# Second product of the first MLP as seven block products in eight steps

## The chip, the cores and the metric

The kernel runs on one core of one Trainium2 chip. The metric is device time in microseconds of one execution; the time before is the median of three runs. A profile is one further execution, recorded by the hardware profiler. Engines are named as the profile names them: PE (TensorE), DVE (VectorE), ACT (ScalarE), POOL (GpSimd) and SP (SyncE, which here only issues transfers).

## The reference

Linear attention with a normalisation gives x of 2304 tokens by 512; then come two MLPs, each 512 to 2048 to 512, the first with softplus, the second with a leaky ReLU.

```
kv  = einsum('bhsd,bhse->bhde', k, v);  o = einsum('bhsd,bhde->bhse', q, kv)
x   = o / sqrt(mean(o*o) + 1e-6) * g_norm          # 4 x 8 x 576 x 64 -> 2304 x 512
h   = x @ w_in                                     # first MLP
x   = (max(h, 0) + log1p(exp(-abs(h)))) @ w_out
h   = x @ w_in2                                    # second MLP
out = max(0.01 * h, h) @ w_out2
```

The MLP weights arrive as float64 and are decoded on the chip to float32.

## The kernel before

**Precision.** Every float32 operand of a matmul is held as two float32r parts, a rounded one and the remainder: ACT copies the value into the first part, and DVE subtracts that from the value for the second (`parts` for the hidden values, lines L908 and L913; `split_part` for x, L785 and L780; `split_w2` for the second product's weights, L676 and L682). One 128x128 block product is then three matmuls: part 0 by part 0, part 0 by part 1, part 1 by part 0.

**Steps.** After the attention stage the MLPs run as 24 steps t, 12 for each MLP: four groups g of 512 of the 2048 hidden features, and in each group three stretches tp of 768 tokens. A step has two half steps s = 2t + u, each with 256 hidden features. A half step's first product, x by w_in, is already seven block products, numbered i = 0 to 6 (`product`, L879, six matmuls each), in place of eight. They are collected in three PSUM banks U, V, W; `after` adds them with ACT (copies out of PSUM, L980) and DVE (adds, L987), applies the activation (L894, L900) and splits the result.

**The second product.** In the first MLP `quarter` and `features` (L1027) multiply the hidden values by w_out, 96 matmuls of 128x384 in a step, collected in banks 4 to 7 and added to `xy` (x and y in turn) by eight DVE adds of 384 columns (`to_xy`, L757). In the second MLP the product is `tokens` (L1043, 512 columns). PE takes turns: a first block product of this step, then pieces of the second product of the step before.

**x.** The seven right sides of the first product (three plain blocks of x, `PLAIN`, and four differences) are kept in DRAM (`xscr`) and loaded again in every step that does not make them. The four differences are stored as split parts, 768 KB each, and loaded by POOL's queue straight into `xe` (L862). The three plain blocks are stored unsplit, 384 KB each, loaded by SP's queue into `xt` (L853), and split again by ACT and DVE in every step. A step whose x is new (`fresh`) makes the parts from `xy`.

**Weights.** A float64 weight tile of 512 per partition is decoded by one ACT instruction (L642) and three DVE ones (a shift L648, two combinations L654 and L660); `split_pair` adds and splits the blocks of w_in (L702, L719, L723).

**Order.** All work is recorded as operations with costs, reads and writes; `Plan.run` places them, engine by engine, from these and from due times. Each engine then runs its list in order. The trace's order is the planner's.

## Time and profile before

| | |
|---|---|
| median of 3 runs | 826.15 us (825.85, 826.15, 827.84) |
| the profiled execution: its time, its span | 827.58 us, 825.8 us |
| PE, DVE, ACT, POOL busy | 812.6, 573.0, 448.7, 66.7 us |
| TensorE clock granted | 0.998 of full speed, 1.00 from 85 us on |
| attention and start | 0 to 85 us |
| first MLP, steps 1 to 11, then second MLP | from 85.1 us, 31.2 us a step; from about 428 us |

The profiled execution's own time is its span and 1.8 us around it. Steps of the first MLP are cut here at multiples of 31.2 us after 85.0 us; three of them (303.4 to 397.0 us) are one group of features, in which every kind of work of the steady state occurs once.

### The profile page before, as it was taken

To read this page: it belongs to the slowest core of one execution; us is meant where nothing else is said; L and a number is where in the kernel's file an instruction comes from. 1 tells how busy PE (TensorE), PEld (TensorE's weight loads), DVE (VectorE), ACT (ScalarE), POOL (GpSimd) and SP (SyncE) were. 2 spreads that over 40 slices of the span, in tenths; PEclk is the share of its full clock that TensorE was granted. 3 is DMA by queue.
4 is the path that set the end of the run, shared out by engine and by line. 5 is a ranking of instruction groups with operands and counts; after the bars stand their busy time and mean duration, and the time that the engine had idled before them with its cause. 6 is when DMAs were issued, how large, how long until landed. Compare 5 with 4: busy or idle time off the path is not lost.

```text
span 825.8 us, 11977 instructions
## 1 busy us (share of the span) xinstructions
PE 812.6 (98%) x4524; PEld 771.8 (93%) x4524; DVE 573.0 (69%) x917; ACT 448.7 (54%) x746; POOL 66.7 (8%) x120
## 2 busy tenths in 40 slices
PE   7899999999999999999999999999999999999997
PEld 6799999999999999999999999899998999999986
DVE  5998888876486756876788875865487765763342
ACT  3777877674464544553566565564365544453330
POOL 3520000010010010010010010010010010010000
PEclk9999999999999999999999999999999999999999
DMA  9991954585275562575585984675455753444513
GB/s 292 319 343 52 356 182 166 180 307 193 99 235 175 189 236 99 189 236 190 217 277 185 328 313 162 223 223 172 150 186 173 241 180 104 164 153 131 174 58 95
DMA packets 78776, 164.08 MB, mean 199 GB/s; under 512 B 11520, under 2 KB 54272, under 8 KB 78720
## 3 DMA queue, kind: packets, MB, share of 16 engines
q1 hardware_dynamic: 67200, 100.42, 35.9%
q0 software_dynamic: 11520, 62.92, 23.5%
q8 instruction: 35, 0.57, 0.3%
q14 instruction: 21, 0.17, 0.1%
HBM read 132.25 MB, written 31.06 MB: 198 GB/s over the span
## 4 chain that ended last, share of the span: by engine, by line
PE 95%; DVE 2%; ACT 1%; DMA 1%; SPq 1%; issue 0%; POOL 0%; ACTq 0%; POOLq 0%
PE ps L879 41%; PE ps L1027 24%; PE ps L1043 24%; PE ps L954 2%; PE ps L501 1%; PE ps L443 1%; PE ps L593 1%; DMA qa<-in_q_dram 1%; PE ps L432 0%; PE ps L509 0%; PE ps L446 0%; DVE mf L702 0%; DVE xy L757 0%; DVE ra L723 0%; DVE xn L571 0%
## 5 line engine op out<-in xcount | busy, mean ns | idle before, releaser
L879 PE MATMUL ps<-ra 128*128 128x384 f32 x1932 | 374.4, 335 | 0.0
L879 PEld LDWEIGHTS ps<-ra 128*128 128x128 f32 x1932 | 340.9, 188 | 5.1
L1027 PE MATMUL ps<-rb 128*128 128x384 f32 x1152 | 226.7, 334 | 0.0
L1043 PE MATMUL ps<-rb 128*128 128x512 f32 x864 | 209.5, 392 | 0.0
L1027 PEld LDWEIGHTS ps<-rb 128*128 128x128 f32 x1152 | 202.1, 188 | 0.0
L1043 PEld LDWEIGHTS ps<-rb 128*128 128x128 f32 x864 | 161.2, 188 | 31.3
L987 DVE TENSOR_TENSOR mf<-ps,mf 128x384 f32<-128x384 f32 x138 | 76.7, 557 | 160.0 <-PE ps L879 153.8
L980 ACT ACTIVATE mf<-ps 128x384 f32<-128x384 f32 x138 | 67.6, 490 | 100.0 <-PE ps L879 98.8
L913 DVE TENSOR_TENSOR rb<-mf,rb 128x768 fp32r<-128x768 f32 x96 | 91.4, 952 | 13.3 <-ACT rb L908 12.7
L757 DVE TENSOR_TENSOR xy<-ps,xy 128x384 f32<-128x384 f32 (+1 forms) x126 | 77.2, 613 | 30.7 <-PE ps L1043 22.2
L862 POOL DMA_DIRECT2D ra<-xscr x80 | 42.4, 530 | 672.9 <-PE ps L879 534.9
L908 ACT ACTIVATE rb<-mf 128x768 fp32r<-128x768 f32 x96 | 81.3, 847 | 2.5
L900 ACT ACTIVATE mf<-mf 128x768 f32<-128x768 f32 (+1 forms) x48 | 32.6, 680 | 76.7 <-DVE mf L987 76.7
L780 DVE TENSOR_TENSOR ra<-mf,ra 128x768 fp32r<-128x768 f32 x63 | 60.2, 955 | 12.7 <-ACT ra L785 12.6
L785 ACT ACTIVATE ra<-mf 128x768 fp32r<-128x768 f32 x63 | 52.9, 839 | 15.2 <-PE ps L879 15.2
L894 ACT ACTIVATE mf<-mf 128x768 f32<-128x768 f32 (+1 forms) x48 | 33.4, 695 | 46.9 <-DVE mf L987 46.8
L752 ACT ACTIVATE xy<-ps 128x384 f32<-128x384 f32 (+1 forms) x36 | 19.0, 528 | 12.6 <-PE ps L1027 11.3
L654 DVE SCALAR_TENSOR_TENSOR sqr<-mf,sqr 128x512 int32<-128x512 int32 x35 | 24.9, 712 | 0.8
L900 ACT ACTIVATE mf<-ps 128x384 f32<-128x384 f32 x24 | 11.8, 491 | 23.9 <-PE ps L879 23.9
L660 DVE SCALAR_TENSOR_TENSOR mf<-mf,sqr 128x512 int32<-128x512 int32 x34 | 24.1, 708 | 0.4
L719 ACT ACTIVATE ra<-mf 128x768 fp32r<-128x768 f32 (+1 forms) x18 | 17.2, 954 | 9.8 <-DVE mf L702 5.5
L642 ACT ACTIVATE mf<-mf 128x512 f32<-128x512 f32 x20 | 13.3, 668 | 14.3 <-DMA mf<-in_moe_w_in_dram 10.6
(97 smaller groups left out, 604.5 us busy)
## 6 DMA issues: line engine op xcount, KB each, us to landing
ra<-xscr POOLq DMA_DIRECT2D x80, 768.0 KB, 5.7
mf<-xscr SPq DMA_DIRECT2D x51, 384.0 KB, 4.6
mf<-in_moe_w_in_dram SPq DMA_DIRECT2D x18, 512.0 KB, 4.6
xscr<-ra SPq DMA_DIRECT2D x12, 768.0 KB, 3.4
xscr<-rc SPq DMA_DIRECT2D x12, 768.0 KB, 5.9
mf<-in_moe_w_out_dram SPq DMA_DIRECT2D x17, 512.0 KB, 4.8
lf<-in_moe_w_out_dram SPq DMA_DIRECT2D x15, 512.0 KB, 3.4
xscr<-xy SPq DMA_DIRECT2D x19, 384.0 KB, 6.1
```

The costliest lines, as they stand in the source:

```text
L757: {"D": t_d(n)}, lambda e: nc.vector.tensor_tensor(dst, src, dst, ALU.add),
L780: ENG[e].tensor_tensor(e_[:, 1, :, :], src(), e_[:, 0, :, :].bitcast(F32), ALU.subtract)
L785: {"A": t_a(n)}, lambda e: nc.scalar.activation(e_[:, 0, :, :], src(), AF.Copy),
L862: lambda e: nc.gpsimd.dma_start(out=flat(xe[i]).ap, in_=xscr[7 * tp + i]),
L879: nc.tensor.matmul(o, w_[:, a, c:c + P], e_[:, b, kk, :], start=(not on and kk == 0 and n == 0), stop=(kk == 1 and n == 2), skip_group_che ...
L900: lambda e: nc.scalar.activation(dst(), src(), AF.Prelu, alpha=0.01),
L908: {"A": t_a(n)}, lambda e: nc.scalar.activation(g[:, 0, :, :], c.ap, AF.Copy),
L913: lambda e: nc.vector.tensor_tensor(g[:, 1, :, :], c.ap, g[:, 0, :, :].bitcast(F32), ALU.subtract),
L980: {"A": t_a(BN)}, lambda e: nc.scalar.activation(c[:, m, :], src, AF.Copy),
L987: lambda e: nc.vector.tensor_tensor(c[:, m, :], src, c[:, m, :], ALU.add),
L1027: nc.tensor.matmul(y[:, :BN], w_[m][:, a, js], G_[:, b, m, :], start=(u == 0 and m == 0 and i == 0), stop=(u == 1 and m == 1 and i == 2),)
L1043: nc.tensor.matmul(y, G_[:, a, m, js], w_[m][:, b, :], start=(u == 0 and m == 0 and i == 0), stop=(u == 1 and m == 1 and i == 2),)
```

## The change

In steps t = 3 to 10 the second product of a step, a 512 by 512 block of w_out by 512 features of 768 tokens, is done as a 2 by 2 scheme of seven block products p (`y_half`, two halves j of 128 output features, six matmuls each) in place of eight. `g_make` forms the right sides from the four blocks of hidden values (c11, c12, c21, c22) with four subtractions and seven splits; `w_parts` forms the left sides from w_out with four sums and seven splits in a group. The products are collected in two pairs of PSUM banks, PX (4, 5) and PY (6, 7): `add` adds a pair to `xy` as 768 columns, `across` copies PX over PY by ACT, and later products accumulate on top. Steps 0 to 2 and 11 keep the eight block products; step 11 takes its weights from `wS`.

In `after` the first product's U is copied by ACT to W (PSUM to PSUM) in place of a copy to SBUF, and product 5 accumulates on it; a DVE add of each half step goes. Where weights are decoded for groups after the first, DVE's shift becomes an ACT instruction. The plain blocks of x are stored split, 768 KB each, and loaded by POOL's queue, without `xt` and without splitting. `ident` and `mask` move to pools that are freed after attention, and all PSUM banks become one tile, `psa`.

```diff
+    cX = Reg("mf", 14 * KI, [2, BN])
+    gS = [Reg("rb", at * KI, [2, 2, BN]) for at in (12, 0, 6, 18)]
+    wS = {
+        p: Reg("rb", at * KI, [2, 2, 256])
+        for p, at in ((5, 52), (3, 48), (1, 32), (6, 36), (7, 40), (2, 44), (4, 28), (0, 24))
+    }
+    gX = Reg("rb", 36 * KI, [2, 2, BN])
+    wsum = Reg("mf", 11 * KI, [2, 256])
...
-    ps = ring(psum, "ps", 8, [P, 512])
+    psa = psum.tile([P, 8, 512], F32, name="psa")
+    ps = [psa[:, i, :] for i in range(8)]
...
+    def strassen(t):
+        return NTP <= t < TL
...
+        if F < GF:
+            op(
+                {"D": t_d(DM, True)},
+                lambda e: nc.vector.tensor_scalar(
+                    t_, a_reg.ap, 3, None, ALU.logical_shift_left
+                ), ak, tk,
+            )
...
+        else:
+            op(
+                {"A": t_a(DM)},
+                lambda e: nc.scalar.activation(
+                    t_, r[:, :, 0].bitcast(mybir.dt.uint32), AF.Copy,
+                    bias=7.5 * 2.0 ** -18 - 0.5, scale=2.0 ** -29 * (1.0 - 2.0 ** -18),
+                ), rk, tk,
+            )
+            op(
+                {"D": t_d(DM)},
+                lambda e: nc.vector.scalar_tensor_tensor(
+                    t_, a_reg.ap, 3, t_, ALU.logical_shift_left, ALU.bitwise_or
+                ), ak + tk, tk,
+            )
...
-    PROD = ((0, 0, 1), (1, 0, 4), (0, 1, 5), (1, 1, 6), (0, 1, 3), (2, 0, 2), (0, 1, 0))
+    PROD = ((0, 0, 1), (1, 0, 4), (0, 1, 5), (1, 1, 6), (0, 1, 3), (2, 1, 2), (0, 1, 0))
...
+    def split_store(tp, i, e_):
+        op(
+            {"S": 2.25},
+            lambda e: nc.sync.dma_start(out=xscr[7 * tp + i], in_=flat(e_).ap.bitcast(F32)),
+            e_.keys(), [("xs", tp, i)],
+        )
...
             src, sk = B(*PLAIN[i])
             if not stages:
                 split_part(xe[i], src, sk)
-            if not stored:
-                x_store(tp, i, src, sk)
+                split_store(tp, i, xe[i])
             return
...
         if i in PLAIN and at_hand:
             split_part(xe[i], *x_block(tp, *PLAIN[i]))
+            split_store(tp, i, xe[i])
             return
...
-        if i in PLAIN:
-            t = xt[xt_no[0] % 2]
-            xt_no[0] += 1
-            op(
-                {"S": 1.2}, lambda e: nc.sync.dma_start(out=t.ap, in_=whole(tp, i)),
-                [("xs", tp, i)], t.keys(),
-            )
-            split_part(xe[i], lambda: t.ap, t.keys())
-            return
...
+    def cs(s):
+        t, u = s // 2, s % 2
+        if not strassen(t):
+            return cA[s % 2], cB
+        return cA[u], (cB, cX)[(t + 1 + u) % 2]
...
         if i == 0:
-            copy(cA_, 1, U, bu)
+            op(
+                {"A": t_a(BN)}, lambda e: nc.scalar.activation(W, U, AF.Copy), bu, bw,
+            )
...
         elif i == 5:
-            plus(cA_, 1, W, bw)
-            act(s, lambda: cA_[:, 1, :], lambda: cA_[:, 1, :], BN, ck(cA_, 1), ck(cA_, 1))
+            act(s, lambda: cA_[:, 1, :], lambda: W, BN, bw, ck(cA_, 1))
         else:
             act(s, lambda: cA_[:, 0, :], lambda: U, BN, bu, ck(cA_, 0))
-            parts(cA_, gA[s % 3])
+            if not strassen(t):
+                parts(cA_, gA_of(s))
...
+    def g_part(t, p, c):
+        g_at[t, p] = g_free.pop(0)
+        parts(c, g_at[t, p])
+
+    def g_minus(dst, a, b):
+        op(
+            {"D": t_s(2 * BN)},
+            lambda e: nc.vector.tensor_tensor(dst.ap, a.ap, b.ap, ALU.subtract),
+            a.keys() + b.keys(), dst.keys(),
+        )
+
+    g_todo = []
+
+    def g_make(t, n):
+        c11, c12 = cs(2 * t)
+        c21, c22 = cs(2 * t + 1)
+        g_todo.extend({
+            6: [(g_part, t, 1, c11), (g_minus, c11, c12, c11), (g_part, t, 5, c11)],
+            11: [(g_part, t, 3, c22)],
+            12: [(g_minus, c11, c22, c11), (g_part, t, 6, c11), (g_minus, c12, c22, c12)],
+            13: [(g_part, t, 7, c12), (g_part, t, 2, c21)],
+            15: [(g_minus, c21, c21, c11), (g_part, t, 4, c21)],
+        }.get(n, ()))
+        g_run()
+
+    def g_run():
+        while g_todo and (g_free or g_todo[0][0] is g_minus):
+            f, *x = g_todo.pop(0)
+            f(*x)
...
+    PX, PY = (4, 5), (6, 7)
+    CHAIN = {1: (PX, 0), 2: (PY, 1), 3: (PY, 1), 4: (PY, 1), 5: (PY, 0), 6: (PX, 1), 7: (PX, 1)}
+
+    def y_half(t, p, j):
+        banks, on = CHAIN[p]
+        bank = banks[j]
+        w_, g_ = wS[p], g_at[t, p]
+
+        def fn(e):
+            for m in range(2):
+                for n, (a, b) in enumerate(((0, 0), (0, 1), (1, 0))):
+                    nc.tensor.matmul(
+                        ps[bank][:, :BN], w_[:, a, m, j * P:(j + 1) * P], g_[:, b, m, :],
+                        start=(not on and m == 0 and n == 0), stop=(m == 1 and n == 2),
+                        skip_group_check=True,
+                    )
+
+        op({"PE": 6 * t_mm[BN]}, fn, w_.keys() + g_.keys(), [("ps", bank)])
+        if j == 0:
+            return
+        g_free.append(g_at.pop((t, p)))
+        g_run()
+        tp = t % NTP
+
+        def pair(b):
+            return psa[:, b[0]:b[1] + 1, :BN]
+
+        def bk(b):
+            return [("ps", x) for x in b]
+
+        def add(dh, k_, b):
+            c0 = (2 * tp + k_) * BN
+            dst = xy[:, 2 * dh:2 * dh + 2, c0:c0 + BN]
+            xk = xyk([2 * dh, 2 * dh + 1], c0, BN)
+            op(
+                {"D": t_s(2 * BN)},
+                lambda e: nc.vector.tensor_tensor(dst, pair(b), dst, ALU.add),
+                bk(b) + xk, xk,
+            )
+
+        def across():
+            op(
+                {"A": t_a(2 * BN)},
+                lambda e: nc.scalar.activation(pair(PY), pair(PX), AF.Copy),
+                bk(PX), bk(PY),
+            )
+
+        if p == 5:
+            add(1, 1, PY)
+        elif p == 3:
+            add(0, 1, PY)
+        elif p == 1:
+            across()
+        elif p == 6:
+            add(0, 1, PX)
+        elif p == 2:
+            add(0, 0, PY)
+            across()
+            add(1, 1, PX)
+        elif p == 4:
+            add(1, 0, PY)
...
+    def w_part(p, src):
+        w_ = wS[p]
+        hk, lk = w_.keys(0, 2048), w_.keys(2048)
+        op(
+            {"A": t_a(DM)},
+            lambda e: nc.scalar.activation(w_[:, 0, :, :], src[0](), AF.Copy), src[1], hk,
+        )
+        op(
+            {"D": t_s(DM)},
+            lambda e: nc.vector.tensor_tensor(
+                w_[:, 1, :, :], src[0](), w_[:, 0, :, :].bitcast(F32), ALU.subtract
+            ), src[1] + hk, lk,
+        )
+
+    def w_sum(dst, a, b, sign):
+        op(
+            {"D": t_s(DM)},
+            lambda e: nc.vector.tensor_tensor(dst[0](), a[0](), b[0](), sign),
+            a[1] + b[1], dst[1],
+        )
+
+    def w_parts(n, last=False):
+        f = w_block
+        S = (lambda: wsum.ap), wsum.keys()
+        R = (lambda: sqr.bitcast(F32).rearrange("p (m n) -> p m n", m=2)), [("sqr",)]
+        if n == 0:
+            w_sum(S, f(1, 0), f(1, 1), ALU.add)
+            w_part(5, S)
+            w_sum(S, S, f(0, 0), ALU.subtract)
+            w_sum(R, f(0, 1), S, ALU.subtract)
+            w_part(3, R)
+        elif n == 1:
+            w_part(1, f(0, 0))
+            if last:
+                w_part(0, f(1, 0))
+        elif n == 2:
+            w_part(6, S)
+            w_sum(S, f(0, 0), f(1, 0), ALU.subtract)
+        elif n == 3:
+            w_part(7, S)
+        elif n == 4:
+            w_part(2, f(0, 1))
+        else:
+            w_part(4, f(1, 1))
+
+    W_AT = {(0, 1): (1,), (0, 3): (2,), (0, 5): (3,), (1, 0): (4,), (1, 2): (5,)}
+    W_FIRST = {(1, 3): (1, 2), (1, 6): (3, 4, 5)}
...
+    SEQ = [(p, j) for p in (5, 3, 1, 6, 7, 2, 4) for j in range(2)]
+    todo = []
...
+                n = 7 * u + i
+                if strassen(t):
+                    g_make(t, n)
+                    if n == 10:
+                        todo += [(t, *x) for x in SEQ]
+                if n < 7 and strassen(t - 1):
+                    g_make(t - 1, 14 + n)
...
+            if not rest:
+                late = len(todo) > 14 + 4 - n if n >= 10 else len(todo) > 10 - n
+                for _ in range(min(len(todo), 1 + late)):
+                    y_half(*todo.pop(0))
+            if t < NT2 and strassen(t):
+                for x in (W_FIRST if g == 1 else W_AT).get((no, i), ()):
+                    w_parts(x, g == NG - 1)
```

**Order on PE.** Two stretches of the first MLP's steady state, `ps` and `psa` being PSUM, `ra` holding x and w_in, `rb` the hidden values and w_out. Before:

```order
L879 MATMUL ps_85<-ra 128x384 x6
L1027 MATMUL ps_87<-rb 128x384 x3
L1027 MATMUL ps_88<-rb 128x384 x3
L879 MATMUL ps_83<-ra 128x384 x6
L1027 MATMUL ps_88<-rb 128x384 x3
L1027 MATMUL ps_89<-rb 128x384 x3
L879 MATMUL ps_85<-ra 128x384 x6
```

After, around the border of steps 6 and 7 (L901 is `product`, L1091 is `y_half`):

```order
L1091 MATMUL psa<-rb 128x384 x24
L901 MATMUL psa<-ra 128x384 x18
L1091 MATMUL psa<-rb 128x384 x12
L901 MATMUL psa<-ra 128x384 x48
L1091 MATMUL psa<-rb 128x384 x12
L901 MATMUL psa<-ra 128x384 x6
L1091 MATMUL psa<-rb 128x384 x24
```

Six matmuls are one block product of the first product or half a block product of the second. The strict turns of before have become runs of up to eight first block products (x48) and of up to four halves (x24).

**Order on DVE.** Both lists stand in the steady state of the first MLP. Before (L757 adds to `xy`, L987 adds in `after`, L913 splits hidden values, L780 splits x):

```order
L757 TENSOR_TENSOR xy<-ps_88,xy 128x384
L913 TENSOR_TENSOR rb<-mf,rb 128x768
L780 TENSOR_TENSOR ra<-mf,ra 128x768
L757 TENSOR_TENSOR xy<-ps_89,xy 128x384
L913 TENSOR_TENSOR rb<-mf,rb 128x768
L757 TENSOR_TENSOR xy<-ps_90,xy 128x384
L987 TENSOR_TENSOR mf<-ps_85,mf 128x384
L987 TENSOR_TENSOR mf<-ps_83,mf 128x384
```

After (L1116 is `add`, L935 a split, L1057 `g_minus`, L1021 an add in `after`, L756 and L735 belong to w_in's blocks):

```order
L1116 TENSOR_TENSOR xy<-psa,xy 128x2x384
L935 TENSOR_TENSOR rb<-mf,rb 128x768
L1057 TENSOR_TENSOR mf<-mf 128x768
L756 TENSOR_TENSOR ra<-lf,ra 128x768
L935 TENSOR_TENSOR rb<-mf,rb 128x768
L1021 TENSOR_TENSOR mf<-psa,mf 128x384
L735 TENSOR_TENSOR lf<-lf 128x256
L1021 TENSOR_TENSOR mf<-psa,mf 128x384
```

The adds to `xy` are wider, the splits of x are gone, and subtractions of 768 columns stand between the adds that free PSUM.

**Order on SP's queue.** The steady state of the first MLP: before, loads of plain x (L853) among the weight loads (L628 for w_in, L633 for w_out):

```order
L633 DMA mf<-in_moe_w_out_dram 128x1024
L633 DMA lf<-in_moe_w_out_dram 128x1024
L853 DMA mf<-xscr 128x768 x5
L633 DMA mf<-in_moe_w_out_dram 128x1024
L853 DMA mf<-xscr 128x768
L633 DMA lf<-in_moe_w_out_dram 128x1024
L628 DMA mf<-in_moe_w_in_dram 128x4x256
```

After (L641 and L646 are the weight loads):

```order
L646 DMA mf<-in_moe_w_out_dram 128x1024
L646 DMA lf<-in_moe_w_out_dram 128x1024
L641 DMA mf<-in_moe_w_in_dram 128x4x256
L641 DMA lf<-in_moe_w_in_dram 128x4x256
L641 DMA mf<-in_moe_w_in_dram 128x4x256
```

Only weights are left there. POOL's loads of x (`ra<-xscr`, 768 KB) are 131 in the whole program where they were 80.

## Rows read from the trace of the kernel before

**Rows 1.** The page: PE over the span, and the chain that ended last.
```profile
PE 812.6 (98%) x4524; PEld 771.8 (93%) x4524; DVE 573.0 (69%) x917; ACT 448.7 (54%) x746; POOL 66.7 (8%) x120
...
PE 95%; DVE 2%; ACT 1%; DMA 1%; SPq 1%; issue 0%; POOL 0%; ACTq 0%; POOLq 0%
```

**Rows 2.** Windows: length, busy time of PE, PEld, DVE, ACT, POOL; clock; DMA.
```profile
303.40:397.00 93.60, 93.60 (x542) 93.60 (x541) 64.24 (x104) 47.27 (x74) 6.33 (x12) 1.00 0.56 185
...
85.00:790.00 705.00, 705.00 (x3813) 672.90 (x3812) 491.94 (x751) 385.23 (x610) 42.40 (x80) 1.00 0.59 198
```

**Rows 3.** Timeline of PE, steady state: start, length, instructions merged.
```profile
345.59 1.20 PE L1027 MATMUL ps<-rb 128*128 128x384 f32 x6
346.63 1.20 PE L879 MATMUL ps<-ra 128*128 128x384 f32 x6
```

**Rows 4.** Groups by line, DVE, 303.4 to 397.0: busy, mean ns, idle before.
```profile
L757 DVE TENSOR_TENSOR xy<-ps,xy 128x384 f32<-128x384 f32 x24 | 13.4, 557 | 3.0 <-PE ps L1027 2.8
L913 DVE TENSOR_TENSOR rb<-mf,rb 128x768 fp32r<-128x768 f32 x12 | 11.4, 951 | 0.4 <-ACT rb L908 0.4
L987 DVE TENSOR_TENSOR mf<-ps,mf 128x384 f32<-128x384 f32 x18 | 10.0, 558 | 24.1 <-PE ps L879 24.1
L780 DVE TENSOR_TENSOR ra<-mf,ra 128x768 fp32r<-128x768 f32 x10 | 9.6, 955 | 0.9 <-ACT ra L785 0.9
...
L648 DVE TENSOR_SCALAR sqr<-mf 128x512 int32<-128x512 int32 x4 | 1.7, 422 | 0.1
...
L682 DVE TENSOR_TENSOR rb<-lf,rb 128x512 fp32r<-128x512 f32 x2 | 1.4, 684 | 0.0
```

**Rows 5.** Groups by line and shape, DVE, whole span.
```profile
L757 DVE TENSOR_TENSOR xy<-ps,xy 128x512 f32<-128x512 f32 x54 | 37.2, 689 | 22.2 <-PE ps L1043 22.2
...
L818 DVE TENSOR_TENSOR mf<-xy 128x768 f32<-128x768 f32 x10 | 9.5, 950 | 0.0
```

**Rows 6.** Groups by line, ACT, 303.4 to 397.0 us.
```profile
L908 ACT ACTIVATE rb<-mf 128x768 fp32r<-128x768 f32 x12 | 10.2, 848 | 0.4
L980 ACT ACTIVATE mf<-ps 128x384 f32<-128x384 f32 x18 | 8.9, 492 | 15.5 <-PE ps L879 15.2
...
L785 ACT ACTIVATE ra<-mf 128x768 fp32r<-128x768 f32 x9 | 7.6, 839 | 4.8 <-PE ps L879 4.8
...
L642 ACT ACTIVATE lf<-mf 128x512 f32<-128x512 f32 x2 | 1.3, 663 | 0.0
...
L676 ACT ACTIVATE rb<-lf 128x512 fp32r<-128x512 f32 x2 | 1.3, 636 | 0.4 <-PE ps L1027 0.4
```

**Rows 7.** Timeline of all engines, 340 to 347 us.
```profile
340.34 1.23 DVE L723 TENSOR_TENSOR ra<-mf,ra 128x1024 fp32r<-128x1024 f32 x1
340.39 1.20 PE L1027 MATMUL ps<-rb 128*128 128x384 f32 x6
340.58 0.49 ACT L980 ACTIVATE mf<-ps 128x384 f32<-128x384 f32 x1 [0.28 <-PE ps L879]
...
342.47 2.24 PE L1027 MATMUL ps<-rb 128*128 128x384 f32 x12
342.74 0.56 DVE L987 TENSOR_TENSOR mf<-ps,mf 128x384 f32<-128x384 f32 x1 [0.57 <-PE ps L879]
```

**Rows 8.** Timelines of ACT and of PE around 26.8 us, in the attention stage.
```profile
26.12 0.68 ACT L581 ACTIVATE xy<-ps,gcol 128x512 f32<-128x512 f32 x1
...
26.86 0.66 PE L593 MATMUL ps<-ident,xn 128*128 128x128 f32 x4 [0.94 <-ACT xy L581]
```

**Rows 9.** Transfers from 303.4 to 397.0 us: total; GB/s in 40 slices; issues, us to landing.
```profile
GB/s 97 381 33 0 0 0 0 0 16 306 403 285 251 337 319 167 4 221 168 67 0 224 155 403 323 180 260 247 281 157 252 46 39 186 11 235 345 425 269 324
DMA packets 5905, 17.35 MB, mean 185 GB/s; under 512 B 463, under 2 KB 2829, under 8 KB 5898
...
ra<-xscr POOLq DMA_DIRECT2D x12, 768.0 KB, 5.6
mf<-xscr SPq DMA_DIRECT2D x8, 384.0 KB, 5.0
```

**Rows 10.** Tile ra from 270 to 310 us: durations in ns, min/median/max, and landings.
```profile
L862 POOL DMA_DIRECT2D ra<-xscr x5: 527/527/530, 272.2 to 303.4; - x5
...
DMA to landing us min/median/max: 4.6/4.7/6.1
```

More of the change, by code (lines that the diff above doesn't have):

```diff
@@ L275, in linear_attention_two_mlps @@
     ]
-    w2s = [Reg("rb", (30 + 4 * i) * KI, [2, DM]) for i in range(NW2)]
+    w2s = [Reg("rb", (32 + 4 * i) * KI, [2, DM]) for i in range(NW2)]
     BN = 384
     NTP = NT // (2 * BN)
+    TL = NG * NTP - 1
     xe = [Reg("ra", 6 * i * KI, [2, 2, BN]) for i in range(7)]
@@ L304, in linear_attention_two_mlps @@
     attp = att.__enter__()
+    ident = mstp.tile([P, P], F32, name="ident")
+    make_identity(nc, ident)
+    mask = attp.tile([P, P], F32, name="mask")
+    nc.vector.memset(mask, 0.0)
+    nc.vector.memset(mask[0:D, 0:D], 1.0)
+    nc.vector.memset(mask[D:P, D:P], 1.0)
     NLD = 5 + 1
@@ L668, in decode_pair, with w2_of @@
             decode_w(F + m, which, half[i][m])
+    def w2_of(f):
+        if f < GF:
+            return w2s[f]
+        return w2s[((5, 4), (0, 3), (1, 2))[(f - NG * GF) // 2 % 3][f % 2]]
     def split_w2(F, i):
         for m in range(2):
-            d_, w_ = half[i][m], w2s[(F + m) % NW2]
+            d_, w_ = half[i][m], w2_of(F + m)
             hk, lk = w_.keys(0, 4 * DM), w_.keys(4 * DM)
@@ L797, in x_store @@
         )
+    def split_store(tp, i, e_):
[4 more added lines that the diff above has]
+        )
     def x_part(tp, i, stages=(), B=None):
-        stored = B is not None
         B = B or (lambda j, k_: x_block(tp, j, k_))
@@ new lines, in linear_attention_two_mlps @@
+    g_free = list(gS)
+    g_at = {}
+    def g_part(t, p, c):
[19 more added lines that the diff above has]
+        g_run()
@@ new lines, in w_block @@
+    def w_block(dh, u):
+        r = sraw[1 - u]
+        return (lambda: r[:, dh::2, :]), part(r, dh) + part(r, dh + 2)
+    def w_part(p, src):
[11 more added lines that the diff above has]
+        )
@@ L1141, in linear_attention_two_mlps @@
         rest = []
-        if t >= 1:
+        if t >= 1 and not strassen(t - 1):
             k_ = 1 - u
@@ L1188, in linear_attention_two_mlps @@
                 split_pair(0, 1)
+        if g + 1 <= NG:
+            if no == 4:
+                decode_pair(F, 1, 1)
+            if no == 5:
+                decode_pair(F + 2, 1, 0)
+                if g + 1 < NG:
+                    w_parts(0)
+                else:
+                    split_w2(F, 1)
+        elif g + 1 < 2 * NG:
+            if no == (2 if g == NG else 0):
+                decode_pair(F, 1, 0)
+            if no == 1 and g > NG:
+                split_w2(F, 0)
+            if no == 5:
                 decode_pair(F + 2, 1, 1)
```

73 lines of the change are left out of this document (33 added, 40 removed).

## The prediction

> **What bounds the kernel now.** Read the page's first and fourth part: PE is busy 812.6 of 825.8 us, and the chain that ended last is 95% PE [rows 1]. The windows then show where: from 85 to 790 us PE is busy for all of 705.00 us at a granted clock of 1.00, and so in the 93.6 us of one group of features, while DVE there is busy 64.24 us, ACT 47.27 and the transfers take 0.56 of the DMA engines' time [rows 2]. A busy PE need not be a PE at its pace, so read the pace from the timeline: one block of six matmuls starts 1.04 us after the one before (345.59, 346.63), 0.173 us a matmul, with no wait noted [rows 3]. A step of 84 + 96 matmuls then needs 31.2 us, which is the 93.6 us over three. PE's instruction count is the time; what DVE and ACT do is free as long as PE never waits for them.
>
> **What is removed from PE.** Eight steps drop from 96 to 84 matmuls of the same shape in the second product: 96 matmuls by 0.173 us are **16.6 us**. The order of the changed kernel has this count, so the saving on PE's list is sure; only waits can eat it. A changed step needs 168 matmuls, 29.1 us, three of them 87.4 us.
>
> **What DVE has to do in it.** All per three steps. In: 9 more splits of hidden values by 0.951 us, 8.6 [rows 4]; 12 subtractions of 768 columns by 0.950 (the nearest row is a difference of x, same shape, SBUF to SBUF), 11.4 [rows 5]; for the weights 3 more splits and 4 sums by 0.684, 4.8 [rows 4]. 24 adds to xy by 0.557 become 18 of 768 columns out of two banks. That shape has no row: the bounds are 0.951, a 768-column subtraction in SBUF [rows 4], and 1.114, two adds of 384; the line through 557 ns at 384 and 689 ns at 512 columns gives 0.953 [rows 4, 5], which I take: 17.2 for 13.4, so 3.8 more (up to 6.7). Out: 9 splits of x by 0.955 (8.6), 6 adds in `after` by 0.558 (3.3), 8 shifts by 0.422 (3.4) [rows 4]. Net +13.3 us: 77.5 us of 87.4, a share of 89% for 69% before. Covered, but the cover shrinks from 9.8 us idle a step to 3.3.
>
> **ACT.** In: 9 splits by 0.848 (7.6), 8 decode instructions by 0.663 (5.3), 3 weight splits by 0.636 (1.9), and 6 copies PX over PY, PSUM to PSUM with 768 columns, without a row: 0.848 and 0.984 (twice 492 ns) are the bounds, 0.85 I take, 5.1. Out: 9 splits of x by 0.839 (7.6). The copy of U stays a copy of 384 columns out of PSUM, now into PSUM [rows 6]. Net +12.3 us, 59.6 of 87.4. No bound.
>
> **Transfers.** Nine loads of 384 KB on SP's queue become nine of 768 KB on POOL's. To 17.35 MB come 3.5 MB, 20.9 MB in 87.4 us or 239 GB/s, where slices of the same window reach 381 to 425 [rows 9]. The room on average is there; each load by itself must land between the last use of its buffer and the next. Before, 14.6 us of PE work lay between (84 matmuls). In the order after, the runs of first block products shorten this to 5.2 us for one load (part 1, from step 6 to 7, inside the run of eight), 8.3 us for four, and 9.3 or more for all others. A landing takes 5.6 us (4.6 to 6.1) [rows 9, 10]: I take **1 us** lost in all, 0 to 2. SP's queue loses what stood ahead of the weight loads; the stores of x (42 of 768 KB for 24, with 4 of 384 KB for 19) sit in steps where x is new, their data are needed a step later at the earliest, and I cost them at nothing: their cover is the 31 us to the next load of that stretch; without it a load comes one landing, some 6 us, late.
>
> **The new waits of PE.** Banks are now handed over more tightly. Take `product` 2, which adds to U only after ACT's copy of U: in a run of first block products only one product, 1.04 us, stands between. Its price reads off the timeline: ACT starts 0.19 us after the next block has started on PE (340.39, 340.58) and takes 0.49; DVE starts 0.27 us after (342.47, 342.74) and takes 0.56 [rows 7]; PE starts 0.06 us after ACT's end at 26.80 [rows 8]. So 0.74 us by ACT and 0.89 by DVE, with 0.30 and 0.15 us to spare, if the engine is free. I count 15 such places in steps 3 to 11 (13 ACT, 2 DVE) in the order after; in the order before the tightest in these steps leaves 3.1 us. An engine that is just in an instruction of 0.85 us makes such a place late, and behind the waiting PE instruction stands all of PE's list. Lower bound 0; upper bound a whole 0.85 us at each, 12.7 us. The planner places them with the other work in view and ACT is idle a third of the time, so I take near the lower end, **2 us**. The seven products p wait for DVE's add or ACT's copy on their pair of banks, but with 2.08 us or more of PE work between for nearly all; queued behind such an add on DVE are the splits and U's adds, which the same 3.3 us of idle time must absorb.
>
> **The rest at nothing.** `ident` and `mask` are the same instructions from another pool, while PE waits for its first loads. The second MLP keeps its matmuls; fewer splits there only leave DVE and ACT idler behind a PE that is busy throughout [rows 2].
>
> **Sum.** 827.6 (the profiled execution's own time) - 16.6 + 2 + 1 = 814.0 us. That execution stands 1.4 us above the median of its runs, so the median forecast is 826.15 - 13.6 = **812.5 us**.
>
> **A rule that speaks against the change.** POOL's issue of a load shows 527 to 530 ns in the steady state, while DVE is 69% busy [rows 2, 10]: no sign that DVE holds it up. The Trainium skill, SBUF — State Buffer, section "SBUF: two separate sides", says that descriptors of a transfer issued by POOL are written by GpSimd's cores, which a DVE instruction in a two-port mode locks out until it ends, and advises the SP or ACT queue; the change does the reverse with 51 loads. The trace does not bear that out so far. As a mechanism of this kernel it would be: each load issued up to one DVE instruction late, 1.23 us for the longest [rows 7]. It costs time only at the five loads with 5.2 or 8.3 us, at most 6 us: 812.5 becomes 814 to 818.
>
> **The rivals.**
> - *Hand-offs late throughout.* DVE, at 89%, comes late to the adds that free PX and PY, once in each of the eight steps by one instruction of 0.95 us, on top of the 15 places: 7.6 us more, 817 to 823. For it: adds stand behind subtractions and splits in DVE's list. Against: DVE still has 3.3 us idle a step, and PE's work can be taken from the other product.
> - *DVE becomes the bound, slower than before.* DVE's idle time does not shrink as needed: in one group 24.1 us of it stood before the 18 instructions of L987, waiting for PE [rows 4], and such waits come from dependences and not from lack of work. A step then lasts 25.8 us (77.5 over 3) plus the idle time that stays. The point from which it decides is 5.4 us a step (31.2 - 25.8); with 7 us it is 32.8 us a step, 8 by 1.6 = 13 us slower, about 839. Against: six of these 18 go with the add that is dropped, and the planner fills the others with the 13.3 us of new work.
> - *POOL's loads locked out*, as above, 814 to 818.
> - That the matmuls are not saved is excluded by the count.
>
> **Chances.** Forecast as summed (809 to 817): 0.76, its own range. Late hand-offs (817 to 823): 0.12. POOL's loads: 0.04. Slower by DVE: 0.06. Something unnamed near the old time: 0.02. No measurement here tells less than 0.3% (2.5 us) from no change; faster by more than that holds the first, the third and nearly all of the second case: 0.90; same 0.03; slower 0.07. The range of 8 in 10 goes from 809 (nothing lost: 826.15 - 16.6 = 809.5, and half a us of scatter) to 821, which takes in waits of 12 us in all and leaves out the upper part of the late hand-offs and the slower case.
>
> **What the profile will show.** L901 and L1091 with the same 1.04 us pace; 168 matmuls in a 29.1 to 30 us step; the matmul count 96 lower. DVE's busy time in three steady steps near 77 us and its waits for PE far below 24 us; `add` near 0.95 us; `across` 0.85 to 0.98 us. In the list of waits, PE waiting for ACT and DVE in many short pieces of under 0.5 us, 2 us in sum, and at the border of steps 6 and 7 one wait of about 0.7 us for a load. The prediction is wrong if PE waits for `add` or for U's adds in every step (late hand-offs), if DVE's busy share in the eight steps reaches 98% (DVE the bound), or if POOL's issues grow beyond 0.53 us and landings beyond 8 us (POOL).

## The result and the profile after

The changed kernel takes **818.44 us** (median of four runs, 814.09 to 819.97) where the kernel before, on the same chip, takes 826.0: a ratio of 0.9892, interval 0.9876 to 0.9909. The forecast of 812.5 was 5.9 us too low; of the 16.6 us of matmuls that go, 7.6 came back as time. The profiled execution after took 819.97 us, 1.5 above the median.

The page after, first, fourth and sixth parts and one group of the fifth, answers to [rows 1, 10]:

```profile
PE 799.8 (98%) x4428; PEld 755.6 (92%) x4428; DVE 559.0 (68%) x836; ACT 463.8 (57%) x791; POOL 93.5 (11%) x171
...
PE 77%; issue 11%; DMA 6%; DVE 2%; ACT 2%; POOL 1%; SPq 1%; POOLq 0%; ACTq 0%; DVEq 0%
PE psa L901 32%; PE psa L1231 22%; PE psa L1091 9%; PE psa L1214 6%; DMA ra<-xscr 2%; DMA lf<-in_moe_w_in_dram 2%; DMA xscr<-rc 2%; PE psa L514 2%; PE psa L456 2%; PE psa L981 2%; POOL ra L884 1%; PE psa L606 1%; DMA qa<-in_q_dram 1%; PE psa L445 1%; PE psa L522 1%
...
L884 POOL DMA_DIRECT2D ra<-xscr x131 | 69.3, 529 | 637.7 <-PE psa L901 566.3
...
ra<-xscr POOLq DMA_DIRECT2D x131, 768.0 KB, 6.6
```

The count of matmuls fell by the 96 forecast, 4524 to 4428. But the chain that ended last is no longer 95% PE: 6% of it are transfers. Next the windows of the changed kernel (columns as in [rows 2]): 147 to 400 us, which holds most of the work with seven products (L1091 runs from 181 to 409 us); 303 to 390 us, three steps of it; and the end of the first MLP.

```profile
147.00:400.00 253.00, 249.96 (x1436) 248.35 (x1435) 208.04 (x279) 160.71 (x261) 29.73 (x56) 1.00 0.66 231
303.00:390.00 87.00, 86.11 (x495) 85.47 (x494) 75.77 (x103) 57.19 (x92) 11.08 (x21) 1.00 0.66 236
400.00:470.00 70.00, 68.10 (x372) 64.67 (x371) 59.87 (x87) 48.20 (x76) 4.22 (x8) 1.00 0.82 296
```

PE, which was busy for all of 705 us [rows 2], now has holes, and more of them at the end of the first MLP, where the transfers reach 296 GB/s. The list of waits names them (PE, 85 to 600 us: us in all, times, longest):

```profile
PE psa L901 <- DMA ra<-xscr: 2.6, 3, 1.7
PE psa L1091 <- ACT psa L1123: 1.2, 3, 0.7
PE psa L1231 <- DVE rb L715: 1.0, 1, 1.0
PE psa L901 <- ACT mf L1014: 0.3, 1, 0.3
PE psa L901 <- ACT psa L1027: 0.2, 1, 0.2
```

These 5.3 us are less than what the holes cost: the wait noted as 1.72 us is 2.02 us from start to start. So the price is read from starts: from the start of a run of n matmuls to the next start, less n times 0.1733 us (0.23 at 512 columns).

| from | next start | lost | PE waits for |
|---|---|---|---|
| 244.82 x12 | 247.36 | 0.46 | `across` (L1123) |
| 260.99 x18 | 264.44 | 0.33 | copy of U (L1027) |
| 264.44 x24 | 270.62 | 2.02 | load of part 1 of x |
| 335.19 x12 | 337.61 | 0.34 | `across` |
| 379.67 x4 | 381.24 | 0.88 | `across` |
| 420.88 x6 | 422.28 | 0.36 | load of x |
| 432.79 x6 | 434.72 | 0.89 | load of x |
| 457.66 x2 | 459.49 | 1.37 | weights of the second MLP (L715) |
| 553.06 x12 | 556.32 | 0.50 | a copy out of PSUM (L1014), itself behind a late weight load (next section) |

Together 7.15 us. The first MLP's first block also starts at 85.70 us instead of 85.07, and from there to the end of the span it is 732.5 us instead of 740.7 (818.2 - 85.70, 825.8 - 85.07). So the MLPs gave back 8.2 of 16.6 us: 8.4 are lost, 7.15 of it in these nine places and 1.3 in smaller ones.

### The profile page after: what moved, and what is told of

Its sections match the earlier page's. It is cut to its first block, busy times and chain, and to the rows that moved or that the text cites. A ratio compares the mean times of both kernels' runs of the same rounds, so it can differ in the third digit from the quotient of the medians.

```text
span 818.2 us, 11611 instructions
## 1 busy us (share of the span) xinstructions
PE 799.8 (98%) x4428; PEld 755.6 (92%) x4428; DVE 559.0 (68%) x836; ACT 463.8 (57%) x791; POOL 93.5 (11%) x171
## 4 chain that ended last, share of the span: by engine, by line
PE 77%; issue 11%; DMA 6%; DVE 2%; ACT 2%; POOL 1%; SPq 1%; POOLq 0%; ACTq 0%; DVEq 0%
PE psa L901 32%; PE psa L1231 22%; PE psa L1091 9%; PE psa L1214 6%; DMA ra<-xscr 2%; DMA lf<-in_moe_w_in_dram 2%; DMA xscr<-rc 2%; PE psa L514 2%; PE psa L456 2%; PE psa L981 2%; POOL ra L884 1%; PE psa L606 1%; DMA qa<-in_q_dram 1%; PE psa L445 1%; PE psa L522 1%
## 5 line engine op out<-in xcount | busy, mean ns | idle before, releaser
L901 PE MATMUL psa<-ra 128*128 128x384 f32 x1932 | 364.9, 335 | 3.2 <-DMA ra<-xscr 2.6
L901 PEld LDWEIGHTS psa<-ra 128*128 128x128 f32 x1932 | 339.6, 188 | 10.9 <-DVE mf L1163 2.0
L1231 PE MATMUL psa<-rb 128*128 128x512 f32 x864 | 211.2, 392 | 1.0 <-DVE rb L715 1.0
L1231 PEld LDWEIGHTS psa<-rb 128*128 128x128 f32 x864 | 161.1, 188 | 32.2 <-DVE rb L715 1.3
L1021 DVE TENSOR_TENSOR mf<-psa,mf 128x384 f32<-128x384 f32 x92 | 50.9, 555 | 114.3 <-PE psa L901 102.1
L935 DVE TENSOR_TENSOR rb<-mf,rb 128x768 fp32r<-128x768 f32 x120 | 113.9, 952 | 21.6 <-ACT rb L930 21.3
L1091 PE MATMUL psa<-rb 128*128 128x384 f32 x672 | 123.6, 335 | 1.2 <-ACT psa L1123 1.2
L1091 PEld LDWEIGHTS psa<-rb 128*128 128x128 f32 x672 | 116.9, 188 | 2.1 <-ACT psa L1123 2.1
L1014 ACT ACTIVATE mf<-psa 128x384 f32<-128x384 f32 x92 | 44.5, 489 | 59.7 <-PE psa L901 58.0
L1214 PE MATMUL psa<-rb 128*128 128x384 f32 x384 | 75.1, 334 | 0.0
L1214 PEld LDWEIGHTS psa<-rb 128*128 128x128 f32 x384 | 67.3, 188 | 0.0
L790 DVE TENSOR_TENSOR xy<-psa,xy 128x512 f32<-128x512 f32 (+1 forms) x62 | 41.5, 671 | 37.0 <-PE psa L1231 36.9
L1116 DVE TENSOR_TENSOR xy<-psa,xy 128x768 f32<-128x768 f32 x48 | 45.7, 955 | 25.9 <-PE psa L1091 24.3
L922 ACT ACTIVATE mf<-mf 128x768 f32<-128x768 f32 x24 | 20.3, 846 | 66.8 <-DVE mf L1021 66.7
L922 ACT ACTIVATE mf<-psa 128x384 f32<-128x384 f32 x48 | 23.1, 482 | 28.9 <-PE psa L901 28.6
L916 ACT ACTIVATE mf<-mf 128x768 f32<-128x768 f32 x26 | 21.9, 843 | 17.3 <-DVE mf L1021 17.3
L1057 DVE TENSOR_TENSOR mf<-mf 128x768 f32<-128x768 f32 x32 | 30.4, 952 | 0.7 <-ACT mf L916 0.3
L916 ACT ACTIVATE mf<-psa 128x384 f32<-128x384 f32 x44 | 21.2, 482 | 12.7 <-PE psa L901 12.5
L1027 ACT ACTIVATE psa<-psa 128x384 f32<-128x384 f32 x46 | 22.0, 478 | 8.3 <-PE psa L901 7.9
```

The costliest lines, as they stand in the source:

```text
L901: nc.tensor.matmul(o, w_[:, a, c:c + P], e_[:, b, kk, :], start=(not on and kk == 0 and n == 0), stop=(kk == 1 and n == 2), skip_group_che ...
L916: {"A": t_a(n)}, lambda e: nc.scalar.activation(dst(), src(), AF.Softplus),
L922: lambda e: nc.scalar.activation(dst(), src(), AF.Prelu, alpha=0.01),
L935: lambda e: nc.vector.tensor_tensor(g[:, 1, :, :], c.ap, g[:, 0, :, :].bitcast(F32), ALU.subtract),
L1014: {"A": t_a(BN)}, lambda e: nc.scalar.activation(c[:, m, :], src, AF.Copy),
L1021: lambda e: nc.vector.tensor_tensor(c[:, m, :], src, c[:, m, :], ALU.add),
```

## The experiments

The medians scatter by some 2 us either way, in large part because the attention stage does: the first MLP's first block starts anywhere from 83.2 to 87.1 us in the profiles of these runs. The table therefore gives beside each time what the MLPs saved against the kernel before in the one profiled execution (740.7 less the span from that first block on). The last column is free of the start, but is one execution each, and the same kernel gave 8.2 and 8.8. Where a time and the pauses of PE disagree about an expectation, the pauses are followed. The runs e1, e2, e3, e7, e9 and e11 leave out part of the computation.

| run | us | ratio, interval | MLPs saved |
|---|---|---|---|
| changed kernel | 818.44 | 0.9892 (0.9876 to 0.9909) | 8.2 |
| e8_after_again | 817.2 | 0.9887 (0.9855 to 0.9919) | 8.8 |
| e1_small_loads | 812.24 | 0.9825 (0.9805 to 0.9846) | 13.9 |
| e2_no_across | 814.75 | 0.9853 (0.9836 to 0.9869) | 10.5 |
| e9_loads_across | 811.72 | 0.9822 (0.9807 to 0.9837) | 15.9 |
| e7_plain_small | 816.23 | 0.9882 (0.9854 to 0.9911) | 9.3 |
| e11_plain_stores | 814.95 | 0.9859 (0.9844 to 0.9874) | 11.8 |
| e3_no_minus | 817.89 | 0.9889 (0.9872 to 0.9906) | 9.5 |
| e4_before_x_split | 826.24 | 0.9992 (0.9981 to 1.0004) | -0.3 |
| e5_margin | 820.21 | 0.9914 (0.9890 to 0.9938) | 8.0 |
| e6_lat | 821.25 | 0.9930 (0.9907 to 0.9953) | 3.8 |
| e10_py_first | 819.15 | 0.9904 (0.9886 to 0.9922) | 6.7 |
| e12_copy_first | 817.85 | 0.9896 (0.9878 to 0.9914) | 9.8 |

**The loads of x.** e1_small_loads:

```diff
-            lambda e: nc.gpsimd.dma_start(out=flat(xe[i]).ap, in_=xscr[7 * tp + i]),
+            lambda e: nc.gpsimd.dma_start(out=flat(xe[i]).ap[:, :16], in_=xscr[7 * tp + i][:, :16]),
```

> The changed kernel with the same order of instructions on every engine, but each of POOL's 131 loads of x moves 16 columns instead of 1536 (the rest of x keeps an older stretch, so this part of the computation is left out). In the changed kernel's trace PE waits 1.7, 0.2 and 0.7 us for loads of x, some 3.3 us with the pauses around them. If loads that land late are the larger part of the lost 9 us, this runs 3.5 to 6 us faster than the changed kernel (812.5 to 815 us). If hand-offs between PE, ACT and DVE are the larger part, it is within 1.5 us of it (817 to 818.5 us).

A load lands in 2.0 us now. The waits of PE that are left (85 to 600 us) are ACT's alone:

```profile
PE psa L1091 <- ACT psa L1123: 1.2, 3, 0.7
PE psa L901 <- ACT psa L1027: 0.2, 1, 0.2
```

Every wait for a load is gone, the late weights at 457 us and the pause at 553 us too, and the MLPs take 5.6 us less than in the changed kernel. The median is 0.3 us below the range expected for late loads. The loads, priced at 1 us, are the larger part of the 8.4 us that are missing.

**The copy PX over PY.** e2_no_across:

```diff
-                lambda e: nc.scalar.activation(pair(PY), pair(PX), AF.Copy),
+                lambda e: None,
```

> The changed kernel with the same order, without ACT's 16 copies from the one pair of PSUM banks to the other (the sums then lack what they carry). PE's pauses before L1091 with ACT L1123 as releaser sum to 1.7 us in the trace. If these waits are worth what the trace shows, 1.5 to 2 us faster than the changed kernel (816.5 to 817 us). If the copies also crowd ACT, so that other hand-offs are late for it, 3 us or more (815.5 us or less). If PE would only wait for the next thing instead, no change.

The three pauses before L1091 are gone, 1.7 us; the load waits stay (1.6 us noted in three pieces), and the load of part 1 alone comes better, 0.7 us lost for 2.0, while the pause at 553 us grows to 1.1 us. By its median, 3.7 us below the changed kernel's, the run would speak for a crowded ACT; but its times go from 812.73 to 818.75 us, and in the profiled execution the MLPs save 2.2 us more, so that case is not shown.

**Both at once.** e9_loads_across makes the two edits together.

> Left out: POOL's loads of x from the scratch are cut to 16 columns each (as in the run with small loads) and the 16 copies of PX over PY on ACT are not made (as in the run without them); matmuls, order and everything else stay. Theory A, that loads and copies together account for what is missing of the 16.6 us: both savings add, about 5.5 + 2 us less than the changed kernel, 809.5 to 811.5 us, and the PE timeline from 85 to 560 us keeps less than 1 us of pauses. Theory B, that something common to all kernels with fewer matmuls is missing as well (a slower pace, the start): not under 812.5 us.

Its windows, to be held against those of the changed kernel:

```profile
147.00:400.00 253.00, 252.83 (x1459) 252.50 (x1458) 211.22 (x283) 149.95 (x245) 29.72 (x56) 1.00 0.23 63
400.00:470.00 70.00, 70.00 (x384) 67.09 (x383) 59.49 (x88) 49.67 (x79) 5.27 (x10) 1.00 0.66 240
```

PE waits once more, 0.17 us for the copy of U, and the MLPs save 15.9 of 16.6 us. The savings add (5.6 by the loads, 2.1 more by the copies). The median, 811.72, is just above the range expected, 0.2 us; that is the start, not PE's pace.

**Which loads, and why.** e7_plain_small cuts only the loads that the change put on POOL's queue, e11_plain_stores their stores on SP's queue as well:

```diff
+            lambda e: nc.gpsimd.dma_start(
+                out=flat(xe[i]).ap[:, :16 if i in PLAIN else 4 * BN],
+                in_=xscr[7 * tp + i][:, :16 if i in PLAIN else 4 * BN],
+            ),
...
+            lambda e: nc.sync.dma_start(
+                out=xscr[7 * tp + i][:, :16 if i in PLAIN else 4 * BN],
+                in_=flat(e_).ap[:, :16 if i in PLAIN else 4 * BN].bitcast(F32),
+            ),
```

> The changed kernel with the same order; only the loads that the change added to POOL's queue (plain blocks, 3 of 7 a step) move 16 columns instead of 1536, so plain x stays old. If the wait at the border of steps 6 and 7 comes from the added loads behind it on the same DMA engines, part 1 lands in 5 to 6 us instead of 7.1, that pause falls from 2.0 to under 0.9 us, and the whole is 2 us or more faster than the changed kernel. If it comes from the gap alone, or from the weights loaded beside it, the pause stays above 1.5 us and the whole is within 1 us.

> Left out: the three plain blocks of x are stored and loaded with 16 columns each, so nearly none of the bytes that the change added move (the run with small plain loads still stored them whole). Theory A, that the added stores on SP's queue, which the forecast costed at nothing, make the loads of step 12 and the weights behind them late: the pauses between 420 and 460 us (0.36, 0.89 and 1.37 us in the changed kernel) fall by 1.5 us or more together, 814 to 815.5 us. Theory B, that they come from the order and the short gaps alone: they stay, 816 to 817 us as with small plain loads. The load pause at 264 us should stay with either, 0.6 to 2 us.

With small loads alone (L904 and L1234 there are L901 and L1231) the pause for part 1 stays, 1.9 us, and the late weights stay, 1.4 us. The median is 2.2 us lower, but the MLPs of the profiled execution save only 1.1 us more. With small stores the end of the first MLP has no pause left; its window and its waits (L907 is L901):

```profile
400.00:470.00 70.00, 70.00 (x385) 67.27 (x384) 60.48 (x89) 48.03 (x76) 4.77 (x9) 1.00 0.75 258
```

```profile
PE psa L907 <- DMA ra<-xscr: 1.7, 1, 1.7
PE psa L1097 <- ACT psa L1129: 1.2, 3, 0.7
PE psa L907 <- ACT psa L1033: 0.2, 1, 0.2
```

So there are three mechanisms. From 420 to 460 us it is the stores that the change added, 2.5 us between the two runs. The chain that ended last in the changed kernel shows how (start, length, what):

```profile
418.34 0.88 DVE rc L813
...
419.28 6.64 DMA xscr<-rc
...
426.46 8.12 DMA ra<-xscr
...
434.72 1.28 PE psa L901 x6
...
446.74 0.97 DVE rc L813
...
447.72 7.45 DMA xscr<-rc
...
455.25 0.85 ACT rc L818
...
458.83 0.61 DVE rb L715
...
459.49 0.50 PE psa L1231
```

A new part of x goes through the staging buffer `rc` to DRAM (6.64 us) and back (8.12), and PE waits at 434.72; the next part may be staged only when the store before it has landed (7.45 us), and behind that waiting split on ACT and DVE stand the splits of the second MLP's weights, for which PE waits at 459.49. The stores from `rc` are not new, but with the added stores small the same load lands in 5.8 us (issued at 424.57 us in e11_plain_stores) and the next store in 3.7 us (at 444.26 us).

At 264 us it is the gap. The timelines of PE, POOL and SP there, in the changed kernel:

```profile
260.99 3.29 PE L901 MATMUL psa<-ra 128*128 128x384 f32 x18
264.44 4.46 PE L901 MATMUL psa<-ra 128*128 128x384 f32 x24 [0.17 <-ACT psa L1027]
270.62 1.11 PE L901 MATMUL psa<-ra 128*128 128x384 f32 x5 [1.72 <-DMA ra<-xscr]
```

```profile
263.53 0.53 POOL L884 DMA_DIRECT2D ra<-xscr  x1 [15.61 <-PE psa L901]
266.06 0.53 POOL L884 DMA_DIRECT2D ra<-xscr  x1 [2.01 <-PE psa L901]
```

```profile
263.30 0.38 SPq L641 DMA_DIRECT2D lf<-in_moe_w_in_dram  x1
```

The load is issued at 263.53, as soon as PE is done with the buffer, and PE continues at 270.62: 7.1 us, where 5.2 us of PE work lie between. With nearly nothing in the loads that the change added it is 7.0 us still (264.89 to 271.87 in e7_plain_small), so these loads do not slow it; with the added stores small as well it is 7.0 us again (261.50 to 268.53 in e11_plain_stores).

At 553 us, in the second MLP, it is the loads that the change added. The wait is noted for ACT, but ACT's copy (L1014) stands behind a weight decode that waited 5.26 us for a load on SP's queue (timeline of ACT):

```profile
555.23 0.66 ACT L655 ACTIVATE mf<-lf 128x512 f32<-128x512 f32 x1 [5.26 <-DMA lf<-in_moe_w_in_dram]
555.79 0.48 ACT L1014 ACTIVATE mf<-psa 128x384 f32<-128x384 f32 x1
```

That load, issued at 540.90 us, lands after 14.2 us; in e7_plain_small, where the added loads are small, after 4.3 us, and PE has no pause there. The issue in the changed kernel, then in e7_plain_small:

```profile
lf<-in_moe_w_in_dram SPq DMA_DIRECT2D x1, 512.0 KB, 14.2
```

```profile
lf<-in_moe_w_in_dram SPq DMA_DIRECT2D x1, 512.0 KB, 4.3
```

**The same kernel again.** e8_after_again, no edit.

> The changed kernel once more, beside the others on one chip. If the lost time sits in fixed places of the order, the pauses of PE are the same to 0.3 us at the same places (2.0 us for part 1 of step 7, 0.9 us before the half product at the end of step 9's sums, 1.4 us for late weights) and the median is 817 to 819.5 us. If they are chance, they differ by a us or more.

Eight of the nine places come back, seven of them to within 0.2 us; the wait for part 1 is 0.56 us for 2.02. The pause at 553 us is missing, and there is one of 1.57 us at 641 us that the first execution did not have: ACT waits 5.40 us there for a weight load that takes 13.3 us, with U's copy behind it. So the pauses from late weights in the second MLP come and go from one execution to the next; the four runs in which the added loads are small have none from 530 us on. The load of part 1, issued at 261.79, is followed by

```profile
267.42 1.28 PE L901 MATMUL psa<-ra 128*128 128x384 f32 x6 [0.25 <-DMA ra<-xscr]
```

that is 5.6 us, with the same issues beside it. One load of this program lands in 5.6 to 7.1 us, and a gap of 5.2 us pays the difference.

**DVE.** e3_no_minus:

```diff
-            lambda e: nc.vector.tensor_tensor(dst.ap, a.ap, b.ap, ALU.subtract),
+            lambda e: None,
```

> The changed kernel with the same order, without the 32 subtractions of hidden values on DVE (30 us of its time in eight steps; the products then get unsubtracted right sides). If DVE's added load (89% of a step by the prediction) makes PE wait, the pauses in steps 6 to 11 shrink and this is 2 us or more faster than the changed kernel (816.5 us or less). If the lost time is loads and single copies, it is within 1 us (817.5 to 819 us).

DVE's work from 147 to 400 us falls from 208.04 to 180.36 us, and PE's time there stays at 249.96: the same pauses at the same places, and 0.3 us more for a load at 356 us. A crowded DVE is not what makes the hand-offs late. From 400 us on the late weights cost only 0.2 us for 1.4, where the store ahead of them landed in 6.3 us for 7.45.

**Split-stored x alone.** e4_before_x_split, the kernel before with that part:

```diff
+                split_store(tp, i, xe[i])
...
-        if i in PLAIN:
-            t = xt[xt_no[0] % 2]
...
-            split_part(xe[i], lambda: t.ap, t.keys())
-            return
```

> The kernel before with one part of the change alone: the three plain blocks of x stored split and loaded by POOL's queue, with eight block products in the second product as before. PE's list is that of before, with 14.6 us between the last use of a buffer and the next. If that part by itself costs nothing, 825.5 to 827 us. If 51 more loads of 768 KB on POOL's queue are late by themselves (locked out, or 35 MB more traffic), 828 us or more.

131 loads on POOL's queue at 534 ns an issue, and no time is lost. The 28 MB of added traffic (35 expected) cost nothing either. In the order of before, with 14.6 us for each load, the stores and loads are free; it is in the new order that PE waits for them. For the rival of POOL's loads locked out this run alone says little, since 14.6 us of cover would hide it. The Trainium skill, SBUF — State Buffer, section "SBUF: two separate sides", warns of it, and no run here shows it (529 ns an issue after, with DVE 82% busy from 147 to 400 us). With DVE's 32 subtractions gone (e3_no_minus) the 131 loads land no sooner, 6.8 us in the median for 6.6.

**The planner's margins.** e5_margin counts more time for a load and a hand-off, e6_lat for a hand-off alone:

```diff
-    LAT = 0.2
+    LAT = 0.3
...
-            {"G": 2.25},
+            {"G": 3.5},
```

> The whole computation of the changed kernel; only two numbers of the planner change: a load by POOL's queue is planned with 3.5 us on the DMA engines in place of 2.25, a hand-off between engines with 0.3 us in place of 0.2. The order then leaves 10.4 us of PE work or more around every load of x (5.2 and 8.3 us before at five places) and 9 instead of 15 hand-offs with a single block product between. If the loads are the larger part of what was lost, their waits go and this is 3 to 5 us faster than the changed kernel. If the planner's order only moves the waits (loads swapped for late copies or late weights), within 1.5 us of it.

> The whole computation; only the planner's hand-off time changes, from 0.2 to 0.3 us. The order then has 10.4 us or more around the loads of steps 4 to 10, and the old 8.3 us around two loads of step 12. If the pause at the border of steps 6 and 7 (2.0 us) and the late copies (2.0 us) are what counts, 2 to 4 us faster than the changed kernel, with the waits for loads of step 12 (1.2 us) kept. If the loads of step 12 and the late weights behind them are what counts, less than 1.5 us faster.

Both missed. e5_margin has no wait for a load left, but PE now waits twice in the second MLP's product for splits of hidden values (1.70 and 0.49 us at 476 us, and the same again at 510 us). e6_lat waits 1.84 us for ACT, and 2.56 us for a copy of ACT's that stands, as at 553 us above, behind a decode waiting for a weight load; more follows (last section). Margins reorder the whole list, and the waits move.

**The late copy at 379.7 us.** The timeline of the changed kernel shows two adds on DVE before it:

```profile
378.28 2.24 PE L901 MATMUL psa<-ra 128*128 128x384 f32 x12
378.48 1.82 DVE L1116 TENSOR_TENSOR xy<-psa,xy 128x768 f32<-128x768 f32 x2 [0.81 <-PE psa L1091]
380.40 0.80 ACT L1123 ACTIVATE psa<-psa 128x768 f32<-128x768 f32 x1 [1.47 <-DVE xy L1116]
...
381.24 0.97 PE L1091 MATMUL psa<-rb 128*128 128x384 f32 x4 [0.72 <-ACT psa L1123]
```

The copy needs only the add of PY. Two small edits of the planner's input, `first` and `after` being further keys that an operation writes or reads:

```diff
 e10_py_first
-            add(0, 0, PY)
+            add(0, 0, PY, first=[("py",)])
...
-            add(1, 1, PX)
+            add(1, 1, PX, after=[("py",)])
 e12_copy_first
-                bk(PX), bk(PY),
+                bk(PX), bk(PY) + [("copied",)],
...
-            add(1, 1, PX)
+            add(1, 1, PX, after=[("copied",)] if t == 9 else ())
```

> The same computation; the planner is only told that product 2's add of PX comes after its add of PY on DVE, which the copy PX over PY waits for. This changes four places in DVE's list and nothing on PE, ACT, POOL and SP. Theory A, that the pause of 0.88 us at 379.7 us comes from the add of PX that DVE does first (0.95 us ahead of the one that ACT waits for): this pause goes, 0.7 to 0.9 us less, 817.3 to 817.8 us if the loads wait as before. Theory B, that the copy is late because PE's product itself ends late: the pause stays at 0.7 us or more and the time at 818.

> The same computation; in step 9 alone the planner is told that product 2's add of PX comes after the copy PX over PY. This moves one add of 768 columns two places down in DVE's list and nothing on PE, ACT, POOL and SP; the copy's wait in the program then names the add of PY, where in the changed kernel and in the run with PY first it names the add of PX that follows it (the two adds stand back to back and one count serves both). Theory A, that this wait for the wrong add makes the pause of 0.88 us at 379.7 us: the copy starts 0.95 us earlier, the pause falls below 0.2 us, and the time by 0.7 to 0.9 us, which is near what the scatter of the start lets one see (817 to 818 us). Theory B, that the copy waits for the product: the pause stays at 0.88 us.

e10 missed: at this place PY's add already stood first (the first add of the two waits for PE, the second for nothing), the two still ran back to back, and the pause stayed, 0.89 us. In e12 the other add stands after the copy; the same stretch:

```profile
376.44 2.25 PE L901 MATMUL psa<-ra 128*128 128x384 f32 x12
376.64 0.96 DVE L1116 TENSOR_TENSOR xy<-psa,xy 128x768 f32<-128x768 f32 x1 [0.81 <-PE psa L1091]
377.63 0.80 ACT L1123 ACTIVATE psa<-psa 128x768 f32<-128x768 f32 x1 [0.55 <-DVE xy L1116]
378.52 1.79 PE L1091 MATMUL psa<-rb 128*128 128x384 f32 x9
```

The copy starts 0.03 us after its add, and PE has no pause. The wait was for the wrong add, 0.95 us too long: in the changed kernel's trace the first of the two adds raises no semaphore, and the second raises DVE's for both. Its median of 817.85 is 0.6 us under the changed kernel's, which the scatter of the start does not let one tell from it.

## Why the prediction held, and where it was mis-sized

The median of 818.44 us lies in the stated range, 809 to 821, but above the 809 to 817 of the forecast's own case, in the stretch that was given to late hand-offs. The runs show that it got there by loads and not by that rival.

- **PE's saving, 16.6 us:** right. With loads and copies out of the way 15.9 us appear.
- **DVE, ACT, transfers:** right. DVE has 75.77 of 87.0 us where 77.5 of 87.4 was forecast, ACT 57.19 for 59.6, the transfers 236 GB/s for 239. The 768-column add takes 955 ns (0.953 forecast); `across` takes 0.79 to 0.81 us, under both bounds (0.848 to 0.984), and the copy of U 478 ns where it was 492.
- **Hand-offs, 2 us (0 to 12.7):** right in kind, and in size partly by luck. The three waits for `across` and the one for U's copy cost 2.0 us. Only the last, 0.33 us, is at a place of the kind that was priced, 15 of them; the other 1.7 us arose where PX and PY are handed over, which was taken as covered by 2.08 us of PE work. In two of these three ACT was in another instruction when the add ended (U's copy at 246.12, a weight decode at 336.20), as had been feared for the 15; in the third the copy waited for a second add. Where it does not wait for it, 2.08 us are just enough (376.44 to 378.52 in e12_copy_first). The waits were not in every step, and DVE at 87% was not their cause, so the rivals of late hand-offs and of DVE as the bound fell.
- **Loads, 1 us (0 to 2):** the term that was mis-sized: 5.6 us by e1, of which five of the nine places are 5.1. The border of steps 6 and 7 was the right place, and its wait 0.6 to 2.0 us for the 0.7 forecast; the landing of 5.6 us was taken from before [rows 9], and after it is 7.1 from 303 to 390 us. The larger part was costed at nothing: "the stores of x ... I cost them at nothing". Their cover, said to be 31 us, does not exist where x is new and passes through `rc`: there the store, the load of the same part, the next staging and the weight splits behind it form one chain, and it cost 2.5 us. The second MLP was costed at nothing too, and SP's queue was said only to lose what stood ahead of the weight loads; but the weights there landed after 14.2 us, with the added loads small after 4.3, which cost 0.5 us in this execution and 1.6 in the next. The rest of the 5.6 us, some 0.5, is in what PE takes to get going again behind each wait and in waits too small to be named.
- **The start, at nothing:** 0.6 us in the profiled execution. The clock was at its lower level there until about 19 us, in the kernel before until about 17 (last section); that the change has no part in it is not shown.

The sum closes: 814.0 forecast for the profiled execution; 4.15 us more of pauses (7.15 for 3), 1.3 of small ones, 0.6 of start make 820.0, and 819.97 was measured.

Open stays why the same load lands in 5.6 us in one execution and 7.1 in the next. A weight load on SP's queue is issued 0.23 us ahead of it in every one of these runs, so its presence alone does not tell them apart; that load was not moved.

## What to carry to other kernels

When PE is the bound and a change takes work from it, everything that was hidden behind that work gets a shorter cover: list each load and store with the PE time that is left between release and use, and price it at the slowest landing in the trace, not the median. A load moved to another queue can hold up the loads that stayed behind (4.3 to 14.2 us here). The stage borders come first, where data are new and stores, loads and staging buffers form chains that a median over steady steps does not show. Before a wait is blamed on a busy engine, look which instruction the wait counts: one that stood behind the needed one cost 0.9 us here.
